# Value slabs on a second DMA queue: a decode-attention kernel with three slab buffers

## The chip, the cores and the metric

The kernel runs on one core of a Trainium2 chip. Its time is the device time of one execution, in microseconds (us), and smaller is better. A core has five engines with a program each, which meet only at semaphores: TensorE (PE) multiplies matrices, VectorE (DVE) and GpSimd (POOL) work element by element, ScalarE (ACT) evaluates functions, and SyncE (SP) does no arithmetic and here issues transfers. A transfer from the chip's main memory (HBM) into the core's own memory (SBUF) is an instruction on one of the engines, which puts the transfer on that engine's queue and goes on; 16 DMA engines then move the bytes, and a semaphore tells when all have landed. SP has a queue (q1 in the profile) and ACT has another (q10).

## The reference

The result is a gated mix of one decode step of attention over a cache and of a small feed-forward network, for two batch rows `b`, in float32:

```python
q = (x @ wq)                          # 640 -> 32 heads x 128
scores = einsum("bhqd,bhkd->bhqk", q, k_cache) * Dh**-0.5     # 4096 cached keys per head
p = softmax(scores)
o = einsum("bhqk,bhkd->bhqd", p, v_cache)
a = o.reshape(B, 1, 32 * 128) @ wo    # -> 640
b = silu(x @ w1) @ w2                 # 640 -> 1728 -> 640
g = sigmoid((x * gate_w).sum(-1))
return g * a + (1 - g) * b
```

Keys and values are 134 MB each, the weights 30 MB together. Every byte is used once.

## The kernel before

**Items.** The attention is cut into 16 items, numbered `i` from 0 to 15: a group of four heads and one batch row each (group `i // 2`, row `i % 2`). The keys of an item are 128 rows of 64 KB, a slab of 8.39 MB that fills one of three equal buffers; its values are another such slab. The text calls them k0 to k15 and v0 to v15. Three loads of weights use the same buffers: the pair of slabs wq (with w1 behind it), the slab mid (two groups of wo, and w2) and, last, the slab end (the other six groups of wo).

**The stream.** The loads have one fixed order, the list `stream` (lines 80 to 88): wq 0, wq 1, k0, v0, k1, v1, ..., k5, v5, k6, mid, k7, v6, k8, v7, ..., k15, v14, v15, end. From k7 on the values are one item behind the keys. `pump` (line 126) goes along this list and issues a load as soon as the entry three places before it has been spent; `spend` marks an entry as done at the place in the program where its last reader stands, and calls `pump`. So the loads stand in the engines' programs at the places of `spend`, and each then waits on the chip for the reader that frees its buffer. The pool `slabs` deals out its three buffers; where two are free at once, it decides which load gets which. In the kernel before, all slab loads are SP's, and SP issues them in the order of the list.

**One item.** Each step is a function. `products(i)`: DVE and POOL multiply the key slab by the query in place, each a part of the columns (lines 346 and 343). `scores(i)`: DVE sums each product over the head dimension (line 354), which spends k_i. `peak(i)`: the negative maximum, four short DVE operations (359 to 363). `weights(i)`: four exps on ACT (369). `total(i)`: PE adds the exps up (380). `values(i)`: 64 matmuls on PE of the exps with the value slab (395), which spends v_i. `combine(i)`: DVE scales the result by the inverse total (407), and PE adds it to the group's rows (417). `turn`: after every second item, DVE sums and transposes a finished group (428, 429). `project` and `merge`: PE multiplies groups by wo (226, 240).

**Order.** The order on each engine is that of the program. The main loop runs i from 0 to 16: products(i), total(i−1), the inverse (`invert`), values(i−1), scores(i), peak(i), weights(i), the query of the next group, then combine(i−1) and turn. So on DVE combine(i−1), which waits for values(i−1), stands ahead of products(i+1). Ahead of the loop stand the gate, the queries (PE, line 314, which spends wq 0) and the first half of the feed-forward network; x and the gate row are loaded by ACT (144, 145). Behind the loop stand the projections with the end slab and one store of 5 KB (479).

**Who frees what.** In the first half v_i takes the buffer of k_(i−1) and waits for scores(i−1) on DVE, and k_i takes that of v_(i−2) and waits for values(i−2) on PE. In the second half v_i takes the buffer of k_i and waits for scores(i), and k_i takes that of v_(i−3) and waits for values(i−3).

Of the kernel before, what the change touches and what calls it, by code (L numbers as in the profile page):

```python
# [15 lines left out]
def tile_gated_decode(  # L16
# [12 lines left out]
    nc = tc.nc  # L29
# [63 lines left out]
    def load_wo(grp, t):  # L93
        at = WO_AT[grp][1]
        src = wo[grp * QD : (grp + 1) * QD, :].rearrange("(p n) d -> p (n d)", n=Q)
        cuts = (0, Q * D - D, Q * D) if grp == HQ - 1 else (0, Q * D)
        for c0, c1 in zip(cuts, cuts[1:]):
            nc.sync.dma_start(t[:, at + c0 : at + c1], src[:, c0:c1])

    def load(what, n, t):  # L100
        if what in ("k", "v"):
            hq, b = items[n]
            src = (kc if what == "k" else vc)[b, Q * hq : Q * hq + Q]
            src = src.rearrange("h s d -> (h s d)").rearrange("(p c) -> p c", p=P)
            step = SLAB // 2 if (what, n) == ("v", N - 1) else SLAB
            for c in range(0, SLAB, step):
                nc.sync.dma_start(t[:, c : c + step], src[:, c : c + step])
        elif what == "wq":
            src = wq.rearrange("(p j) n -> p (j n)", j=J)
            if n == 0:  # L110
                nc.sync.dma_start(t, src[:, :SLAB])
            else:
                nc.sync.dma_start(t[:, :W1_AT], src[:, SLAB:])
                nc.sync.dma_start(t[:, W1_AT : W1_AT + J * F], w1.rearrange("(p j) f -> p (j f)", j=J))
        elif what == "mid":
            for grp in range(WO_MID):
                load_wo(grp, t)
            nc.sync.dma_start(t[:, : FR * D], w2[:FM, :].rearrange("(p n) d -> p (n d)", n=FR))
            nc.sync.dma_start(
                t[:, W2T_AT : W2T_AT + HD], w2[FM:, :].rearrange("r (e c) -> (r e) c", e=2)  # L120
            )
        else:
            for grp in range(WO_MID, HQ):
                load_wo(grp, t)

    def pump():
        while nxt[0] < len(stream):
            m = nxt[0]
            if m >= SLOTS and stream[m - SLOTS] not in spent:
                return  # L130
            t = slabs.tile([P, SLAB], F32, tag="slab", name=stream[m][0])
            load(*stream[m], t)
            T[stream[m]] = t
            nxt[0] += 1
# [38 lines left out]
    for i in range(2):  # L173
        t = const.tile([P, NG, 32], F32, name=f"pz{i}")
# [328 lines left out]
```

## Time and profile before

| | |
|---|---|
| median of 3 runs | 700.46 us (699.23 to 700.59) |
| profiled execution: its time | 700.36 us |
| its span, first to last instruction | 698.5 us |
| bytes read from HBM | 298.26 MB, 427 GB/s over the span |
| busy: DVE / PE / POOL / ACT | 469.4 / 224.7 / 265.7 / 37.8 us |
| TensorE clock granted, mean | 0.667 |

How the lines are read. The rows of slices cut the span in 40 equal parts of 17.5 us; a digit is the busy share in tenths, and 9 is 90% or more. A row of the queue table has the queue's packets, megabytes and the time its packets took as a share of 16 engines' span. A row of the timeline has the start in us, the length in us, the engine (SPq and ACTq are the issues of transfers), the line, the operation, what it writes and what it reads, and in brackets the engine's idle time before it and what ended that. A row of groups has the busy time, the mean in ns of one, and the idle time of the engine before such instructions. A row of windows has the stretch, its length, the busy time of each engine, the granted clock, the share of the DMA engines and GB/s. The landing of a transfer is read from the first instruction that waited for it.

### The profile page before, as it was taken

How to read it: one execution, taken by the hardware profiler on the slowest of the kernel's cores; microseconds unless marked ns; L12 is line 12 of the kernel's file. 1: busy time of each engine (PE TensorE's matmuls, PEld its weight loads, DVE VectorE, ACT ScalarE, POOL GpSimd, SP SyncE). 2: the span in 40 equal slices, each digit the busy share in tenths (PEclk: the TensorE clock that was granted, in tenths of full speed). 3: DMA queues.
4: the chain of work that ended last, by engine and by line, in shares of the span. 5: the costliest groups of instructions: out<-in, count | busy, mean ns of one | idle time of the engine just before them, and what ended most of it. 6: DMA issues, size and time to landing. Idle time of an engine off the chain costs nothing.

```text
span 698.5 us, 3649 instructions
## 1 busy us (share of the span) xinstructions
PE 224.7 (32%) x1516; PEld 73.4 (11%) x1516; DVE 469.4 (67%) x215; ACT 37.8 (5%) x143; POOL 265.7 (38%) x27
## 2 busy tenths in 40 slices
PE   1630050605032150752240506050321406060477
PEld 1210010101010010210010102010100102010113
DVE  2016949394967869496949597695949495786901
ACT  0000000101010100101010101000010101010010
POOL 1006244270907153353618080624426080715300
PEclk9985565756657575877575757566565757566689
DMA  9999999999999999999999999999999999999995
GB/s 410 408 454 424 420 455 439 420 428 440 443 428 432 424 448 435 413 446 439 424 440 432 439 428 440 428 435 435 436 432 432 435 424 448 428 440 424 425 416 248
DMA packets 6803, 298.51 MB, mean 427 GB/s; under 512 B 759, under 2 KB 895, under 8 KB 1154
## 3 DMA queue, kind: packets, MB, share of 16 engines
q1 hardware_dynamic: 6780, 298.26, 98.8%
q8 instruction: 12, 0.20, 0.1%
q14 instruction: 5, 0.04, 0.0%
q10 hardware_dynamic: 6, 0.01, 0.0%
HBM read 298.26 MB, written 0.01 MB: 427 GB/s over the span
## 4 chain that ended last, share of the span: by engine, by line
DMA 60%; DVE 24%; PE 13%; another core or an unknown queue 1%; ACT 0%; issue 0%; SPq 0%; DVEq 0%; ACTq 0%
DMA k<-in_A_k_cache_dram 34%; DMA v<-in_A_v_cache_dram 20%; DVE s L354 15%; PE pv L395 10%; DVE k L346 8%; DMA wq<-in_B_w_dram 5%; PE acc L226 2%; PE orow L417 1%; PE hr L257 1%; DVE osb L407 0%; ACT pz L369 0%; PE tot L380 0%; DVE rg L388 0%; DVE m L359 0%
## 5 line engine op out<-in xcount | busy, mean ns | idle before, releaser
L343 POOL TENSOR_TENSOR k<-k,qsb 128x7680 f32<-128x7680 f32 x16 | 262.8, 16422 | 386.4 <-DMA k<-in_A_k_cache_dram 386.4
L354 DVE TENSOR_REDUCE s<-k 128x68 f32<-128x8704 f32 (+1 forms) x32 | 276.3, 8677 | 0.0
L346 DVE TENSOR_TENSOR k<-k,q 128x8704 f32<-128x8704 f32 x16 | 147.5, 9221 | 136.5 <-DMA k<-in_A_k_cache_dram 126.4
L395 PE MATMUL pv<-v,pz 128*32 128x512 f32 x1024 | 145.2, 730 | 247.9 <-DMA v<-in_A_v_cache_dram 247.9
L395 PEld LDWEIGHTS pv<-v,pz 128*32 128x32 f32 x1024 | 36.5, 131 | 342.7 <-issue 226.7
L417 PE MATMUL orow<-osb,pick 128*128 128x512 f32 x32 | 22.8, 800 | 117.4 <-DVE osb L407 117.4
L369 ACT ACTIVATE pz<-s,nb 32x128 f32<-32x128 f32 x64 | 25.5, 398 | 585.2 <-DVE nb L363 584.6
L407 DVE SCALAR_TENSOR_TENSOR osb<-pv,rg,own 128x512 f32<-128x512 f32 x16 | 12.0, 748 | 21.3 <-PE pv L395 21.2
L276 DVE STREAM_TRANSPOSE turned<-hr 128x416 f32<-128x416 f32 (+1 forms) x2 | 0.8, 414 | 29.4 <-PE hr L265 29.4
L380 PE MATMUL tot<-rs,fold 128*128 128x1 f32 x32 | 5.8, 251 | 43.9 <-ACT pz L369 43.9
L417 PEld LDWEIGHTS orow<-osb,pick 128*128 128x128 f32 x32 | 5.8, 226 | 127.1 <-DVE osb L407 127.1
L331 PE MATMUL q<-qrow,spread 128*128 128x128 f32 x32 | 7.2, 359 | 26.1 <-DVE tot L385 17.8
L314 PE MATMUL qr<-wq,xz 128*32 128x512 f32 x80 | 11.5, 745 | 8.7 <-DMA wq<-in_A_wq_dram 8.7
L428 DVE TENSOR_REDUCE row<-orow 128x128 f32<-128x512 f32 x8 | 5.5, 692 | 11.6 <-PE orow L417 11.6
L380 PEld LDWEIGHTS tot<-rs,fold 128*128 128x128 f32 x32 | 7.2, 235 | 55.3 <-ACT pz L369 52.3
L226 PE MATMUL acc<-mid,hT 128*17 128x320 f32 x52 | 10.0, 556 | 7.6 <-DMA mid<-in_B_w_dram 7.6
L369 ACT ACTIVATION_READ_ACCUMULATOR pz<-s,nb 32x1 f32 x64 | 11.8, 184 | 0.0
L226 PE MATMUL acc<-end,oP 128*17 128x320 f32 (+2 forms) x128 | 11.2, 367 | 0.0
L331 PEld LDWEIGHTS q<-qrow,spread 128*128 128x128 f32 x32 | 5.4, 240 | 33.0 <-issue 22.9
L478 DVE COPY ot<-acc 128x160 f32<-128x160 f32 x1 | 0.3, 324 | 11.0 <-PE acc L226 11.0
L257 PE MATMUL hr<-wq,xz 128*32 128x416 f32 x40 | 5.6, 681 | 3.7 <-DMA wq<-in_B_w_dram 3.7
L197 DVE COPY xz<-xT 128x10 f32<-128x10 f32 x1 | 0.2, 168 | 9.1 <-PE xT L189 9.1
(59 smaller groups left out, 69.0 us busy)
## 6 DMA issues: line engine op xcount, KB each, us to landing
v<-in_A_v_cache_dram SPq DMA_DIRECT2D x2, 4096.0 KB, 38.3
end<-in_A_wo_dram SPq DMA_DIRECT2D x5, 1280.0 KB, 21.3
wq<-in_B_w_dram SPq DMA_DIRECT2D x1, 4320.0 KB, 37.2
mid<-in_B_w_dram SPq DMA_DIRECT2D x1, 4160.0 KB, 26.8
mid<-in_A_wo_dram SPq DMA_DIRECT2D x2, 1280.0 KB, 17.4
wq<-in_A_wq_dram SPq DMA_DIRECT2D x1, 2048.0 KB, 26.5
end<-in_A_wo_dram SPq DMA_DIRECT2D x1, 960.0 KB, 27.0
end<-in_A_wo_dram SPq DMA_DIRECT2D x1, 320.0 KB, 27.3
```

The source lines that it names most:

```text
L226: nc.tensor.matmul(dst[32 * n : 32 * n + m, :], lhsT, w[:, n * width : (n + 1) * width], start=(count[to] == 0), stop=(count[to] == total_ ...
L257: nc.tensor.matmul(rows[32 * c : 32 * c + 32, :QF], xz[:, j, :], w[:, j, c * QF : (c + 1) * QF], start=(j == 0), stop=(j == J - 1),)
L314: nc.tensor.matmul(ps[u][32 * q : 32 * q + 32, :], xz[:, j, :], w[:, u * half : (u + 1) * half, q, :], start=(j == 0), stop=(j == J - 1),)
L331: nc.tensor.matmul(qps[hq][:, b, :], spread[:, b, :], qrow[:, hq, :], start=True, stop=True)
L343: nc.gpsimd.tensor_mul(k[:, CV:, :], k[:, CV:, :], qsb[hq][:, b, None, :].to_broadcast([P, C - CV, DH]))
L346: nc.vector.tensor_mul(k[:, :CV, :], k[:, :CV, :], qps[hq][:, b, None, :].to_broadcast([P, CV, DH]))
L354: nc.vector.reduce_sum(S[i][:, c0:c1], k[:, c0:c1, :], axis=AX.X)
L369: nc.scalar.activation(pz[i % 2][lo:hi, :, 4 * q : 4 * q + 4], S[i][lo:hi].rearrange("p (g c) -> p g c", c=4), AF.Exp, bias=M[i][lo:hi], s ...
L380: nc.tensor.matmul(t[:, :1], fold.rearrange("p a q c -> p (a q c)"), R[i], start=True, stop=True)
L395: nc.tensor.matmul(PV[i][32 * q : 32 * q + 32, :], pz[i % 2][:, gr, :], v[:, gr, :], start=(gr < 4), stop=(gr >= NG - 4),)
L407: nc.vector.scalar_tensor_tensor(osb, PV[i].rearrange("p (c d) -> p c d", d=DH), R[i], own[:, :, None].to_broadcast([P, 4, DH]), op0=ALU.mult,
L417: nc.tensor.matmul(PO[hq].rearrange("p c d -> p (c d)"), pick[:, HB * (1 - b) : HB * (1 - b) + P], osb.rearrange("p c d -> p (c d)"), star ...
```

## The change

Value loads are issued by ACT on its queue instead of by SP. Keys and weights stay with SP.

```diff
             for c in range(0, SLAB, step):
-                nc.sync.dma_start(t[:, c : c + step], src[:, c : c + step])
+                eng = nc.sync if what == "k" else nc.scalar
+                eng.dma_start(t[:, c : c + step], src[:, c : c + step])
```

A line is added, so lines behind 107 count one more in the changed kernel. In the built program, 17 loads (v15 is loaded in two halves) move from SP's program into ACT's. Each v_i stands on ACT at the place of the `spend` that lets it out: v0 ahead of the query copies, v1 to v5 and v6 to v14 each ahead of the four exps of `weights` of the item that was just scored, v15 behind v14. On SP the keys and the weights follow each other directly.

The waits of most loads are as before. From v7 on the pool, which there has two free buffers for two loads at the same place, deals them the other way round:

| load | waits before | waits after |
|---|---|---|
| v1 to v6 | DVE, scores(0) to scores(4), scores(6) | the same |
| k2 to k8, mid | PE, values(0) to values(5), middle; DVE, scores(5) | the same |
| v7 to v14 | DVE, scores(i) | PE, values(i−1) |
| k9 to k15 | PE, values(i−3) | DVE, scores(i−2) |
| v15 | PE, values(13) | DVE, scores(14) |
| end | DVE, scores(15) | PE, values(14) |

So in the changed kernel v6 to v14 and the end slab use one and the same buffer, and k7 to k15, with mid and v15, the other two. The last piece of the end slab also waits for the first half of v15, with which it shares a semaphore.

## The prediction

> **What bounds the kernel now.** I read the slices first, then the queue table, then the timeline around the slab loads.
>
> ```profile
> span 698.5 us, 3649 instructions
> DMA  9999999999999999999999999999999999999995
> ...
> DMA packets 6803, 298.51 MB, mean 427 GB/s; under 512 B 759, under 2 KB 895, under 8 KB 1154
> ...
> q1 hardware_dynamic: 6780, 298.26, 98.8%
> ...
> q10 hardware_dynamic: 6, 0.01, 0.0%
> ```
>
> Transfers bound it: SP's queue (q1) keeps the 16 DMA engines at 98.8% of the span, and only the last slice is not full. ACT's queue (q10) carries nothing but x and the gate. A load of 128 rows makes 128 packets and, as the 759 small ones show (47 such loads times 16 are 752), a completion mark on each of 16 engines. So moving the same bytes can win almost nothing; the question is whether the DMA engines, with two queues, ever run empty.
>
> ```profile
> 0.74 0.39 SPq L111 DMA_DIRECT2D wq<-in_A_wq_dram  x1
> 1.30 0.23 ACTq L145 DMA_DIRECT2D wq<-in_gate_w_dram  x1
> 10.59 2.33 PE L189 MATMUL xT<-ident,wq 3*128 3x3 f32 x10 [10.59 <-DMA wq<-in_gate_w_dram]
> 22.96 11.55 PE L314 MATMUL qr<-wq,xz 128*32 128x512 f32 x80 [8.66 <-DMA wq<-in_A_wq_dram]
> 32.85 0.33 SPq L107 DMA_DIRECT2D v<-in_A_v_cache_dram  x1
> 58.18 9.22 DVE L346 TENSOR_TENSOR k<-k,q 128x8704 f32<-128x8704 f32 x1 [10.06 <-DMA k<-in_A_k_cache_dram]
> 67.44 17.28 DVE L354 TENSOR_REDUCE s<-k 128x68 f32<-128x8704 f32 x2
> 84.74 0.33 SPq L107 DMA_DIRECT2D v<-in_A_v_cache_dram  x1
> 88.43 9.53 PE L395 MATMUL pv<-v,pz 128*32 128x512 f32 x64
> 97.00 9.22 DVE L346 TENSOR_TENSOR k<-k,q 128x8704 f32<-128x8704 f32 x1 [11.23 <-DMA k<-in_A_k_cache_dram]
> 98.03 0.33 SPq L107 DMA_DIRECT2D k<-in_A_k_cache_dram  x1
> ```
>
> What to see: k0 has landed at 58.18, DVE has its scores at 84.72 (26.6 later), and v1, which takes k0's buffer, is issued at once, 12.3 us before k1 lands (97.00). That lead is what keeps the engines fed with three buffers.
>
> ```profile
> 391.53 0.33 SPq L107 DMA_DIRECT2D v<-in_A_v_cache_dram  x1
> 392.60 0.33 SPq L107 DMA_DIRECT2D k<-in_A_k_cache_dram  x1
> 394.58 0.69 DVE L428 TENSOR_REDUCE row<-orow 128x128 f32<-128x512 f32 x1 [1.22 <-PE orow L417]
> 403.30 9.22 DVE L346 TENSOR_TENSOR k<-k,q 128x8704 f32<-128x8704 f32 x1 [7.59 <-DMA k<-in_A_k_cache_dram]
> 422.71 9.64 PE L395 MATMUL pv<-v,pz 128*32 128x512 f32 x64 [27.63 <-DMA v<-in_A_v_cache_dram]
> ...
> 430.07 0.33 SPq L107 DMA_DIRECT2D v<-in_A_v_cache_dram  x1
> 432.41 0.33 SPq L107 DMA_DIRECT2D k<-in_A_k_cache_dram  x1
> 442.00 9.22 DVE L346 TENSOR_TENSOR k<-k,q 128x8704 f32<-128x8704 f32 x1 [8.83 <-DMA k<-in_A_k_cache_dram]
> ```
>
> The second half: v8 and k10 are issued a microsecond apart, on scores(8) and values(7), while k9 is still in transfer. One period is 442.00 − 403.30 = 38.7 us for two slabs, 19.35 us each (8.39 MB, 434 GB/s). Each DMA engine carries 8 of a slab's 128 rows, 2.42 us a row.
>
> ```profile
> 636.24 9.22 DVE L346 TENSOR_TENSOR k<-k,q 128x8704 f32<-128x8704 f32 x1 [6.34 <-DMA k<-in_A_k_cache_dram]
> 663.01 3.48 SPq L98 DMA_DIRECT2D end<-in_A_wo_dram  x7
> 674.82 6.44 PE L395 MATMUL pv<-v,pz 128*32 128x512 f32 x32 [4.29 <-DMA v<-in_A_v_cache_dram]
> 683.20 9.07 PE L226 MATMUL acc<-end,oP 128*17 128x320 f32 x72
> 695.80 0.69 SPq L479 DMA_DIRECT2D out_dram<-ot  x1
> ```
>
> The tail: the end slab, queued last, lands last.
>
> ```profile
> 690.00:698.50 8.50, 4.76 (x88) 2.53 (x84) 0.32 (x1) 0.42 (x1) 0.00 (x0) 0.95 0.15 60
> ```
>
> The engines carry it for 0.15 of the last 8.5 us (the column before GB/s), so to about 691.3, and some 7 us follow. The out row puts a bound on a transfer's fixed cost: 695.80 to the span's end is 2.7 us for 5 KB. I take 2.65 in all, of which 0.95 lies between issue and first row and 1.7 between last row and use.
>
> **The change part by part.** *Issue slots.* 17 value loads leave SP and join ACT at about 0.33 us each, 5.6 us. ACT is idle beside them:
>
> ```profile
> L369 ACT ACTIVATE pz<-s,nb 32x128 f32<-32x128 f32 x64 | 25.5, 398 | 585.2 <-DVE nb L363 584.6
> ```
>
> So they cost nothing. Were that cover gone, it would be 5.6 us. What stands behind a waiting load on ACT is the next weights (four exps, 2 us), whose reader, PE, waits for the value slab anyway. SP loses the same slots and waits for keys alone.
>
> *How two queues share.* No run here has two slab streams, but the start has two queues. The gate row, issued on ACT at 1.53, is used at 10.59, in the middle of the 8 MB weight load queued before it (used at 22.96). x and gate make six entries on q10 by the queue table (three rows, three completion marks); if a row of x and the gate's row meet on one engine, four of them stand there in line, and four turns against rows of 2.42 us are 9.7 us: 1.5 + 9.7 = 11.2 against 10.59 measured. So I take it that an engine serves the two queues in turn, one row each: two slab loads together run at half speed each. With that rule, the waits of the built program and the durations above I walk the loads forward.
>
> The Trainium skill ("DMA: Bandwidth & Descriptors", "Queues, rings and completion order") says the same of the turns, but that one holds a whole packet of some 9 to 17 descriptors, which could be all 8 rows of a slab with their mark. The gate row speaks for single rows; by the packet rule the time would be that of the first rival.
>
> *Start.* v0 is issued at 33 as before, but now shares with k0 rather than waiting behind it. v0's 8 rows all go before k0's last, so k0 is ready 19.35 us later, at 77.5. Scores(0) end 26.6 later at 104.1, and v1's first row is at 105.0. k1's last row has gone at 97.00 − 1.7 = 95.3, since the bytes before it are the same; k2 waits for values(0), behind scores(0). Nothing is left to move: a hole of 9.7 us. Through items 1 to 6 the walk finds at most 0.5 us more: value and key loads overlap, each lands later, and each next issue still finds the other queue busy.
>
> *The buffers, from v7 on.* Here two loads are requested at one place in the code with two free buffers, and the built program deals them out otherwise than before: each of v7 to v14 takes the buffer of the value load before it (waits for values(i−1) on PE), and each of k9 to k15 that of the key load two before (waits for scores(i−2)). So values have one buffer, keys two. A value load can't be in transfer while the values before it are read: each must land (1.7), be read (8.5 to 9.6 by the rows above, 9.0 taken) and be issued anew (0.95 and some 0.3), 12 us in which only keys can move.
>
> The walk repeats every two items. v7 is used by 425.4; only then does DVE pass combine(7) and the turn of a finished head group (3 us), products and scores take 27, and k11 goes out at about 456.3. Meanwhile v8 starts at 426.6, shares with k10's last rows for some 7 us and is gone at 451.1. DVE holds both key slabs, PE needs v8 to land: a hole of 5.2 us. In the next item k11 and v9 overlap, k12 comes in time, and there is none. So two items take 82.8 instead of 77.4 us, with three holes (behind v8, v10, v12): 15.6 us.
>
> *End.* After k15 the only slabs left are v14, v15 and end. v14 waits for values(13); v15's buffer (k14's) has been free since scores(14), but it stands behind v14 in ACT's order. v13's last row goes at 660.8, v14's first row comes 1.7 + 9.0 + 0.3 + 0.95 later: 11.9 us of hole. The tail behind the end slab stays as it is, 0.
>
> *Sum.* 9.7 + 0.5 + 15.6 + 11.9 = 37.7 us. The profiled execution took 700.36, 0.1 from the median of 700.46, so 738. Bounds: with 0.7 and 2.7 us for the landing instead of 1.7 the walk gives +32 and +44, with values at 8 and 10 us +34 and +42; rows of 2.40 or 2.44 us move it by under 2. Both kinds together give its own range, 728 to 750.
>
> **The rivals.** *Whole loads in turn, or the later holes absorbed.* If an engine finishes a load before it changes queue, k0 still waits out v0, 9.7 us; but a later value load is done in one slab's time, half a period sooner, and the walk then finds no hole: 710. The same comes out if buffers turn out not to bind. Against it: the gate row. 0.14.
>
> *Service in order of issue across queues.* k0 then keeps its place and the start costs nothing; the one value buffer still costs 2.1 to 2.6 us in every second late item, under a microsecond in those between and 11.6 at the end, together 20: 720. Against it: the gate row again, in use 12 us before the load issued ahead of it. 0.05.
>
> *One queue gets more turns.* If ACT's goes first each time, the walk finds three holes of 10 us in the first three items, and k15 lands behind all other slabs but one, so that its products and scores (27 us) stand at the very end, some 25 us longer: 756. Nothing in the rows of before speaks for such an order. 0.05.
>
> *Faster: two queues move more bytes per second.* It would have to make up for the holes, 37.7 us of 698.5, so the rate must rise from 434 to over 459 GB/s at one point, the transfers themselves.
>
> ```profile
> GB/s 410 408 454 424 420 455 439 420 428 440 443 428 432 424 448 435 413 446 439 424 440 432 439 428 440 428 435 435 436 432 432 435 424 448 428 440 424 425 416 248
> ```
>
> No slice passes 455, and high ones stand beside low ones (408, 454, 424), as when packets fall to one side of a slice's edge; the engines already count as full. At 465 GB/s all the time it would be about 690. 0.03. The Trainium skill ("DMA: Bandwidth & Descriptors", "Specifications") gives a ceiling of 435 GB/s, which the 434 here agrees with; that would leave nothing to gain.
>
> *No change.* Order of service by issue, and buffers that never bind: 700.4. 0.02.
>
> **How the numbers follow.** My forecast, holes at start, late items and end, has 0.71: 738. Left out of 710 to 750 are the 756 case, faster, no change, and tails of the forecast and the first rival, together some 0.18. About 0.2% (1.4 us) is what a measurement here tells from no change. Only the no-change case lies within it, and only the rate case below it: faster 0.03, same 0.02, slower 0.95.
>
> **What will show it.** Right: DVE's first products on k at about 77 instead of 58.18; the DMA row below 9 in the slices at 94 to 104, near 453, 536, 619 and from 661 to 672; the share of q1 about half, q10 the other, together some 94%; v loads issued on ACT right after PE's values, from v7 on; v14 and v15 issued together near 672; the end slab last, near 731. Wrong on sharing: k0 at 58, or v0 used long before k0. Wrong on buffers: a v and a k load issued within 2 us of each other all through the second half, as now. Most likely to upset it: a fixed cost of a transfer other than 2.65 us, which counts at every hole.

## The result, and the profile after

The changed kernel takes 746.46 us (745.48 to 747.54, 4 runs) beside 700.45 for the kernel before: a ratio of 1.0665, 95% interval 1.0653 to 1.0677. The ratio is taken over all executions and is not exactly the quotient of the two medians. The changed kernel is 46.0 us slower; 37.7 were forecast, with 738 for the time and a range of 710 to 750.

The page of the changed kernel, with the slices of the DMA engines and its queues:

```profile
span 745.3 us, 3645 instructions
DMA  9999949997999999999999997999989996975995
GB/s 394 452 405 447 450 172 448 397 451 338 448 397 447 450 392 447 417 448 429 436 441 429 426 443 296 397 450 450 394 339 447 419 429 282 450 338 241 433 418 235
...
q1 hardware_dynamic: 4332, 164.04, 51.3%
q10 hardware_dynamic: 2454, 134.23, 41.9%
```

The unbroken row of nines now has dents in six places. The two queues together keep the engines at 93.2%, where one kept them at 98.8%, with the same megabytes. The dents in the changed kernel's windows, with GB/s as the last column:

```profile
90.00:110.00 20.00, 2.80 (x14) 1.09 (x18) 19.85 (x7) 1.96 (x8) 17.05 (x2) 0.50 0.50 203
...
175.00:195.00 20.00, 7.50 (x48) 2.60 (x52) 17.66 (x10) 1.96 (x8) 9.95 (x2) 0.59 0.86 360
200.00:300.00 100.00, 25.18 (x146) 8.23 (x147) 76.63 (x30) 6.44 (x26) 34.52 (x3) 0.61 0.99 428
450.00:470.00 20.00, 11.30 (x70) 3.46 (x70) 12.98 (x7) 1.02 (x5) 0.00 (x0) 0.64 0.67 276
532.00:552.00 20.00, 10.56 (x69) 3.43 (x70) 13.34 (x7) 0.70 (x3) 0.00 (x0) 0.64 0.77 315
614.00:634.00 20.00, 9.46 (x68) 2.98 (x68) 15.35 (x7) 0.09 (x1) 0.00 (x0) 0.64 0.65 266
660.00:680.00 20.00, 9.87 (x66) 2.42 (x66) 4.78 (x7) 0.57 (x3) 15.75 (x1) 0.69 0.51 207
730.00:745.30 15.30, 11.57 (x137) 5.21 (x136) 1.43 (x3) 0.42 (x1) 0.00 (x0) 0.97 0.46 194
```

Between the holes the rate is what it was (428 over 100 us). At 434 GB/s a stretch of 20 us with 203 lacks 20 × (1 − 203/434) = 10.6 us of transfer, whether the engines were empty or slow; the six come to 10.6, 3.4, 7.3, 5.5, 7.7 and 10.5, together 45.0. Each of these is uncertain by a microsecond or two, since a window may cut through the rows of 64 KB; their sum stands well beside the span's 46.8 us more.

The timeline of the changed kernel around the holes:

```profile
77.53 9.22 DVE L347 TENSOR_TENSOR k<-k,q 128x8704 f32<-128x8704 f32 x1 [24.12 <-DMA k<-in_A_k_cache_dram]
97.02 16.48 POOL L344 TENSOR_TENSOR k<-k,qsb 128x7680 f32<-128x7680 f32 x1 [2.95 <-DMA k<-in_A_k_cache_dram]
104.10 0.36 ACTq L108 DMA_DIRECT2D v<-in_A_v_cache_dram  x1
...
185.07 16.52 POOL L344 TENSOR_TENSOR k<-k,qsb 128x7680 f32<-128x7680 f32 x1 [10.05 <-DMA k<-in_A_k_cache_dram]
185.76 0.33 ACTq L108 DMA_DIRECT2D v<-in_A_v_cache_dram  x1
...
422.12 9.39 PE L396 MATMUL pv<-v,pz 128*32 128x512 f32 x64 [34.52 <-DMA v<-in_A_v_cache_dram]
431.58 0.34 ACTq L108 DMA_DIRECT2D v<-in_A_v_cache_dram  x1
434.61 9.18 DVE L347 TENSOR_TENSOR k<-k,q 128x8704 f32<-128x8704 f32 x1
458.47 9.98 PE L396 MATMUL pv<-v,pz 128*32 128x512 f32 x64 [24.02 <-DMA v<-in_A_v_cache_dram]
461.33 0.33 SPq L108 DMA_DIRECT2D k<-in_A_k_cache_dram  x1
...
669.17 8.75 PE L396 MATMUL pv<-v,pz 128*32 128x512 f32 x64 [32.83 <-DMA v<-in_A_v_cache_dram]
677.99 1.32 ACTq L108 DMA_DIRECT2D v<-in_A_v_cache_dram  x3
700.23 8.58 PE L396 MATMUL pv<-v,pz 128*32 128x512 f32 x64 [18.38 <-DMA v<-in_A_v_cache_dram]
708.87 3.31 SPq L98 DMA_DIRECT2D end<-in_A_wo_dram  x7
742.61 0.68 SPq L480 DMA_DIRECT2D out_dram<-ot  x1
```

k0 is used at 77.53 instead of 58.18. k1 has landed by 97.02, as before, but v1 is asked for only at 104.10, when scores(0) are done: in the kernel before it was asked for 12.3 us ahead of k1's landing, now 7.1 us behind. In the second half PE's values(7) end at 431.5, and in that instant v8 is issued; v8 lands at 458.47, and the next load of any kind is k11 at 461.33. At the end v13 lands at 669.17, and v14 and v15 are issued together at 677.99, right after values(13).

### The profile page after: what moved, and what is told of

It reads as the page before. It is cut to its first block, busy times and chain, and to the rows that moved or that the text cites. A ratio compares the mean times of both kernels' runs of the same rounds, so it can differ in the third digit from the quotient of the medians.

```text
span 745.3 us, 3645 instructions
## 1 busy us (share of the span) xinstructions
PE 225.0 (30%) x1516; PEld 71.6 (10%) x1516; DVE 468.7 (63%) x215; ACT 37.8 (5%) x143; POOL 266.0 (36%) x27
## 3 DMA queue, kind: packets, MB, share of 16 engines
q1 hardware_dynamic: 4332, 164.04, 51.3%
q10 hardware_dynamic: 2454, 134.23, 41.9%
## 4 chain that ended last, share of the span: by engine, by line
DMA 61%; PE 18%; DVE 15%; another core or an unknown queue 3%; issue 1%; ACT 0%; SPq 0%; DVEq 0%; ACTq 0%
DMA v<-in_A_v_cache_dram 42%; PE pv L396 14%; DMA k<-in_A_k_cache_dram 14%; DVE s L355 9%; DMA wq<-in_B_w_dram 6%; DVE k L347 5%; PE acc L227 1%; PE hr L258 1%; PE orow L418 1%; DVE osb L408 0%; ACT pz L370 0%; PE tot L381 0%; DVE m L360 0%; DVE turned L277 0%
## 5 line engine op out<-in xcount | busy, mean ns | idle before, releaser
L332 PE MATMUL q<-qrow,spread 128*128 128x128 f32 x32 | 5.6, 299 | 6.5 <-DVE tot L386 6.5
L227 PEld LDWEIGHTS acc<-end,oP 128*17 128x17 f32 (+1 forms) x128 | 5.1, 98 | 6.4 <-issue 6.1
```

The lines of the kernel that those rows point to most:

```text
L227: nc.tensor.matmul(dst[32 * n : 32 * n + m, :], lhsT, w[:, n * width : (n + 1) * width], start=(count[to] == 0), stop=(count[to] == total_ ...
L332: nc.tensor.matmul(qps[hq][:, b, :], spread[:, b, :], qrow[:, hq, :], start=True, stop=True)
```

## The experiments

Each kernel's median stands beside that of the kernel before on the same chip (699.8 to 700.3). Edits are shown against the changed kernel, but for one that starts from the kernel before. Where a kernel has three fixed buffers, the line of the three pools is shown in the first experiment only.

### The start alone

Three pools of one buffer each replace the pool of three, so that entry m of the stream takes buffer m mod 3 and all waits are those of the kernel before. Only v0 goes to ACT.

```diff
-    slabs = ctx.enter_context(tc.tile_pool(name="slabs", bufs=SLOTS))
+    slabs = [ctx.enter_context(tc.tile_pool(name=f"slab{s}", bufs=1)) for s in range(SLOTS)]
...
-            t = slabs.tile([P, SLAB], F32, tag="slab", name=stream[m][0])
+            t = slabs[m % SLOTS].tile([P, SLAB], F32, tag="slab", name=stream[m][0])
...
-                eng = nc.sync if what == "k" else nc.scalar
+                eng = nc.scalar if what == "v" and n == 0 else nc.sync
```

> The start by itself: three fixed buffers, v0 alone on ACT, every other load on SP. My theory: k0 is used at 77 to 78, one hole of 9.7 to 10.7 us after k1, and nothing else since one queue follows: 709 to 712 us. If the hole after k3 (4 us in the changed kernel) also comes from the start alone: up to 715. Rival 'the start costs less than its hole, the later order wins some back': 703 to 707.

Measured: 710.97 us against 700.32, ratio 1.0154 (1.0140 to 1.0168), so 10.7 us for one load on the other queue. Its windows show one hole and full rate behind it:

```profile
90.00:110.00 20.00, 2.88 (x14) 1.10 (x18) 19.85 (x7) 1.96 (x8) 17.12 (x2) 0.50 0.52 210
110.00:300.00 190.00, 60.97 (x396) 19.56 (x392) 138.63 (x54) 10.91 (x43) 68.98 (x5) 0.65 1.00 433
300.00:690.00 390.00, 124.98 (x800) 38.40 (x792) 289.57 (x112) 21.08 (x84) 164.21 (x10) 0.65 1.00 434
```

The first term of the sum (9.7 us) is shown, and the smaller hole near 185 is not part of it. Its queue rows (94.9% and 2.7% of a span of 708.1 us) say that the packets took 691.1 us, 1.0 more than the 98.8% of 698.5 us before; this is taken up with the sum below.

### How the queues share

One column of v0 is copied by DVE as soon as v0 has landed.

```diff
+    mark = const.tile([P, 1], F32, name="mark")
+    nc.vector.tensor_copy(mark, T["v", 0][:, :1])
     for i in range(N + 1):
```

> The changed kernel with one added DVE copy of one column of v0, ahead of the first products, where DVE is idle: it starts when v0 has landed. My theory (one row of each queue in turn): v0 and k0 run together from 33 on, v0 is read at 70 to 74, k0 at 77 to 78. Rival 'an engine finishes a load before it changes queue': v0 at about 56, k0 at 77. Rival 'in order of issue': v0 at about 77, k0 at 58. The time stays at 746.

```profile
76.25 0.15 DVE L457 COPY mark<-v 128x1 f32<-128x1 f32 x1 [22.28 <-DMA v<-in_A_v_cache_dram]
77.55 9.22 DVE L347 TENSOR_TENSOR k<-k,q 128x8704 f32<-128x8704 f32 x1 [1.15 <-DMA k<-in_A_k_cache_dram]
```

v0, issued 30 us behind k0, lands 1.3 us ahead of it: both ran side by side to the end. Whole loads in turn (56) and service in order of issue (k0 at 58) are out.

The 70 to 74 that I expected are missed by 2 us, and yet single rows in turn are right. The trace keeps a record of every packet, with its queue, size, start and length. From 45 to 70 us 81 rows of 64 KB start on SP's queue and 80 on ACT's, so neither queue gets more turns. On 14 of the 16 engines v0's last row has ended by 71.3, as the rule says. But on 12 of them the completion mark comes only at 73.2 to 73.7, which fits a turn of its own behind one more row of k0 (2.42 us). On two engines v0's last row ends at 75.7, and the semaphore waits for these. The time was 745.2 in its one execution.

### The buffers with two queues

The changed kernel with the three fixed buffers, all value loads on ACT:

```diff
-            t = slabs.tile([P, SLAB], F32, tag="slab", name=stream[m][0])
+            t = slabs[m % SLOTS].tile([P, SLAB], F32, tag="slab", name=stream[m][0])
```

> The changed kernel, but the three buffers are three pools and entry m of the stream takes buffer m mod 3, so that the loads wait as in the kernel before: v_i for scores(i), k_i for values(i-3). All value loads stay on ACT. My theory: the hole after k1 (9.7 us) stays, the late holes are gone: 710 to 716 us, the upper end if items 1 to 6 hold another 4 us as the changed kernel's profile suggests. Rival 'two slab streams at once are slow whatever the buffers': about 746. Rival 'the start costs nothing': about 700.

Measured: 717.65 (715.25 to 721.02), ratio 1.0256 (1.0216 to 1.0296), above the 710 to 716 expected. Of 46 us, 28 go with the buffers alone; the forecast had 15.6 + 11.9 = 27.5 for that.

The same part from the other side: v0 to v6 on SP, so the start and the first items are those of the kernel before; v7 to v15 on ACT, and the pool deals the buffers again (v7 to v14 in one).

```diff
-                eng = nc.sync if what == "k" else nc.scalar
+                eng = nc.sync if what == "k" or n <= MID + 1 else nc.scalar
```

> The late part by itself: v0 to v6 on SP, v7 to v15 on ACT, and the pool deals the buffers as in the changed kernel, v7 to v14 in one buffer. Against e8 (707.4), which has the same queues and fixed buffers, the difference is the one value buffer with two queues. My theory: three holes of 5 us, one of 12 and what e8 loses: 727 to 737. Rival 'the buffer only matters when the early loads have already spent the lead': 707 to 712.

Measured: 729.48 (726.77 to 731.29), ratio 1.0414 (1.0388 to 1.0439), 29.2 us; its windows hold the largest hole at the end, as in the changed kernel:

```profile
475.00:495.00 20.00, 10.47 (x66) 2.56 (x66) 12.64 (x8) 1.90 (x8) 16.70 (x2) 0.68 0.76 315
...
640.00:660.00 20.00, 9.62 (x66) 2.40 (x66) 11.77 (x8) 1.22 (x5) 15.53 (x1) 0.71 0.41 161
```

So the value buffer needs no spent lead at the start to cost. The kernel with the same queues and fixed buffers (late values on ACT, below) loses 7.6 us, so here the one value buffer is worth some 22 of the 29 us, less than the 28 beside early values on ACT.

### The buffers with one queue

The kernel before, all loads on SP, with three pools and the changed kernel's deal:

```diff
+    def slot_of(m):
+        what, n = stream[m]
+        if what == "k" and n > MID + 2:
+            return 0 if n % 2 == 0 else 1
+        if what == "v" and n > MID + 1:
+            return 0 if n == N - 1 else 2
+        return 2 if what == "end" else m % SLOTS
...
+            t = slabs[slot_of(m)].tile([P, SLAB], F32, tag="slab", name=stream[m][0])
```

> The kernel before, all loads on SP, but from v7 and k9 on the buffers are dealt out as in the changed kernel: v7 to v14 follow each other in one buffer, k9 to k15 alternate in the other two, and end takes the value buffer. My theory: with one queue the loads keep their order and are requested some 11 us before the engines need them, values(i-1) end within 2 us of scores(i), so 700 to 702 us: the one value buffer costs only together with the second queue. Rival 'one value buffer costs by itself, since a value load can't be in transfer while the values before it are read': about 727.

Measured: 700.23 against 700.00, ratio 1.0001 (0.9992 to 1.0011). No change. The same three buffers in the same deal cost 28 us with two queues and nothing with one. With one queue the values are done within 2.4 us of the scores (the timeline of before, 430.07 and 432.41), and a slab asked for then still stands behind others: here v8 is issued at 432.02, and k9, ahead of it on the queue, is used at 442.11, 10 us later.

### The other queue by itself

Three fixed buffers, every slab load on ACT in the order of the stream, x and the gate on SP:

```diff
-                eng = nc.sync if what == "k" else nc.scalar
+                eng = nc.scalar
...
-                nc.sync.dma_start(t, src[:, :SLAB])
+                nc.scalar.dma_start(t, src[:, :SLAB])
...
-    nc.scalar.dma_start(xg[:B], x.rearrange("b s d -> (b s) d"))
+    nc.sync.dma_start(xg[:B], x.rearrange("b s d -> (b s) d"))
```

> Three fixed buffers; all slab loads, keys, values and weights, are issued by ACT in the order of the stream, on one queue, and x and the gate by SP: the same single queue as before, but the other one. If ACT's queue, its issue slots between the exps or its program order cost anything, it shows here: over 703. My theory, that only the meeting of two queues costs: 700 to 702 us.

```profile
q10 hardware_dynamic: 6768, 298.26, 98.9%
```

Measured: 699.16 against 699.82, ratio 0.9990 (0.9981 to 0.9998). ACT's queue is as good as SP's, and its issue slots among the exps cost nothing. A tenth of a per cent is less than this measurement can tell from no change, so this is no better kernel.

### What is left without either hole

v0 on SP and three fixed buffers; 16 of 17 value loads stay on ACT.

```diff
-                eng = nc.sync if what == "k" else nc.scalar
+                eng = nc.sync if what == "k" or n == 0 else nc.scalar
```

> Both of the two former edits: v0 on SP, three fixed buffers, 16 of 17 value loads on ACT's queue. My theory: no hole is left, the DMA engines stay full, 699 to 702 us, no change from the kernel before although almost all value loads still share the engines with the keys. Rival 'ACT's queue, its issues or the interleaving of rows cost something by themselves': over 706. Rival 'two queues move more bytes per second': under 698.

Measured: 710.43 (704.24 to 713.83), ratio 1.0139 (1.0081 to 1.0197). My theory was wrong here: some 10 us remain, and single executions lie 10 us apart, where the kernels with one queue stay within 2. The profiled one (708.05, a span of 706.1) loses 1.8 us between 130 and 140, where v2 is issued at 133.28 with little left to move, and nothing in the long late stretch:

```profile
130.00:140.00 10.00, 4.98 (x20) 1.84 (x24) 8.06 (x7) 2.33 (x9) 3.19 (x1) 0.53 0.87 354
375.00:600.00 225.00, 58.91 (x392) 17.94 (x396) 170.78 (x65) 12.22 (x49) 96.86 (x6) 0.63 1.00 434
```

Its queue rows show more of it:

```profile
q1 hardware_dynamic: 4476, 172.43, 56.8%
q10 hardware_dynamic: 2310, 125.84, 41.5%
```

Together these are 694.1 us of 706.1, so the same packets took 4.0 us longer than in the kernel before. Its packet records have three groups of some 15 slow rows, near 134, 213 and 366 us, each where a value load starts as the load before it runs out.

So I supposed that the rest stood in items 1 to 6, where k_i lands later for the rows of v_i in between. Two kernels split it, both with fixed buffers:

v7 to v15 on ACT (the late values):

```diff
-                eng = nc.sync if what == "k" else nc.scalar
+                eng = nc.sync if what == "k" or n <= MID + 1 else nc.scalar
```

> Three fixed buffers as in e2; v0 to v6 on SP behind the keys, only v7 to v15 on ACT. It halves what is left in e3 (about 10 us over the kernel before, with no v0 at the start and no shared value buffer). My theory of that rest: as long as v_i is issued while k_i is still in transfer, k_i lands later by the rows of v_i that go in between, and the 12 us by which a load is requested ahead shrinks to nothing in items 1 to 6 (small holes of 1 to 2 us near 137, 292), while from item 7 on the rate is full (434 GB/s from 375 to 600 us in e3) and only the end loses some 3 us. So here 702 to 705 us. Rival 'two slab streams slow the engines everywhere': 706 to 708.

v1 to v6 on ACT (the early values):

```diff
-                eng = nc.sync if what == "k" else nc.scalar
+                eng = nc.scalar if what == "v" and 0 < n <= MID + 1 else nc.sync
```

> The other half: three fixed buffers, v1 to v6 on ACT, v0 and v7 to v15 on SP. My theory: the lost lead of items 1 to 6 stands here, 703 to 708 us, and the small holes near 137 and 292 are seen again. Rival 'the rest is at the end': 700 to 701.

Measured: late 707.41 (701.28 to 709.19), ratio 1.0089 (1.0058 to 1.0120); early 704.59 (702.45 to 708.79), ratio 1.0079 (1.0051 to 1.0108). Both halves cost, and both vary. The early values came out as expected, the late ones at the rival's 706 to 708: that the early items hold it all is refuted. The late kernel's profiled execution was its fastest (701.28), so no profile shows where 707 comes from; this part stays open.

The changed kernel with v0 given back to SP, buffers as the pool deals them:

```diff
-                eng = nc.sync if what == "k" else nc.scalar
+                eng = nc.sync if what == "k" or n == 0 else nc.scalar
```

> The changed kernel with one load given back: v0 is issued by SP behind k0, all other value loads by ACT. The waits of the late loads are those of the changed kernel (one value buffer from v6 on). My theory (queues served row by row, and the value buffer): k0 is used at 58 again, the hole after k1 is gone, the late holes (about 5, 5, 5 and 12 us) stay: 727 to 733 us. Rival 'sharing alone does it, buffers never bind': about 700. Rival 'the late part does it all': about 746.

Measured: 742.44 (734.82 to 743.59), ratio 1.0583 (1.0530 to 1.0636). Only some 4 us come back, and I had expected 13 to 19. Its DMA slices:

```profile
DMA  9999999999999999999999995999699995975996
```

The hole at the start is gone, and k0 is used at 58.87 again. But the dents of the second half are deeper: 5, 6, 5 and 5 tenths, where the changed kernel has 7, 8, 6 and 5. By its packet records the four late holes are empty for 8.2, 7.0, 7.4 and 11.9 us, beside 5.7, 4.2, 5.9 and 10.5. With v1 on ACT k1 comes at 107.22 (97.00 in the kernel before), so the keys run later against the values from there on; that this deepens the late holes is not shown. The parts are not independent, and 10.7 us for v0 by itself is not what it costs among the rest.

### Two details of the late part

v15 on SP, where it doesn't stand behind v14:

```diff
-                eng = nc.sync if what == "k" else nc.scalar
+                eng = nc.sync if what == "k" or n == N - 1 else nc.scalar
```

> The changed kernel with both halves of v15 issued by SP, so that they no longer stand behind v14 in ACT's order; their buffer has been free since scores(14). As the prediction words it, v15's place behind v14 is why 12 us pass empty near 670: then the hole closes, and 734 to 736 us. Rival, the same walk done again for this case: the hole only moves, for v15 now shares with v14 and the end slab, which follows in v14's buffer, has to wait for values(14) with no other transfer left: 744 to 748, no change, with a hole of 12 us near 708 instead of 670.

```profile
660.00:680.00 20.00, 10.80 (x66) 2.62 (x66) 2.67 (x6) 1.38 (x6) 16.46 (x1) 0.66 0.96 414
700.00:720.00 20.00, 11.91 (x84) 3.68 (x88) 9.95 (x8) 1.96 (x8) 0.00 (x0) 0.72 0.37 147
```

Measured: 744.33, ratio 1.0661 (1.0601 to 1.0722), as the changed kernel. The hole near 670 closes, and 13 us open near 710, ahead of the end slab, which waits for values(14) in the one value buffer. ACT's order was the place of the hole, not its cause.

The query copy ahead of the waiting load. In the changed kernel the waits show it:

```profile
DVE k L347 <- ACT qsb L334: 8.4, 4, 2.1
```

```diff
+            if i + 1 < N and items[i + 1][1] == 0:
+                query(items[i + 1][0])
             scores(i)
             peak(i)
             weights(i)
-            if i + 1 < N and items[i + 1][1] == 0:
-                query(items[i + 1][0])
```

> The changed kernel with the query of the next group computed ahead of scores(i): on ACT its copy then stands ahead of the waiting value load and the four exps, not behind them. In the changed kernel products of every second item wait 2.1 us for that copy. Rival 'the copy behind the load costs time': faster by up to 8 us (four times 2.1), 738 to 744. My walk: products, scores and so the key loads of even items come 2 us sooner and are used up sooner beside the value load, so each of the three late holes grows by 2 to 3 us: 748 to 754.

Measured: 747.95 (746.39 to 752.52), ratio 1.0708 (1.0672 to 1.0743). Not faster, so the four waits of 2.1 us cost nothing. The 748 to 754 of the walk are not clearly met either: the median stands at their lower edge, and the interval meets that of the changed kernel.

## Why the prediction was right

**Bound and sign.** Transfers bound the kernel, nothing was to be won, and most of the loss is time in which the DMA engines have nothing to move. The rule of single rows in turn is borne out by the packet records (81 and 80 rows in 25 us). The mean rate between holes, 428 to 434 GB/s, is that of one queue, and the rival of a higher rate falls. The Trainium skill ("DMA: Bandwidth & Descriptors", "Issuing engines are not separate DMA queues") says that queues of several engines interleave on the same 16 engines and save only issue time. The trace agrees that nothing is saved; what is lost by the interleaving is on top of that.

**Start: 9.7 us, right.** k0 was to be ready at 77.5 and is used at 77.53; scores(0) at 104.1, v1 issued at 104.10. By landings the hole is 104.10 − 97.02 + 2.65 = 9.7, and alone it costs 10.7.

**Items 1 to 6: 0.5 us, mis-sized.** By landings it is 185.76 − 185.07 + 2.65 = 3.3 us. v3 was asked for when scores(2) were done, and k2 had been used only at 158.6. The prediction does not show this part of its walk, so which of its landings came too early stays open. Two things that it left out make a shared load land later: the mark's own turn, and the longer first rows told below. The early sharing costs 4.8 us by itself in the kernel with early values on ACT.

**Late holes: 15.6 us, right in kind and nearly in size.** v8's landing to k11's issue is 461.33 − 458.47 = 2.9, with 2.65 some 5.5 us. The rows for v10 and v12:

```profile
541.21 9.58 PE L396 MATMUL pv<-v,pz 128*32 128x512 f32 x64 [24.40 <-DMA v<-in_A_v_cache_dram]
543.70 0.33 SPq L108 DMA_DIRECT2D k<-in_A_k_cache_dram  x1
...
624.54 8.87 PE L396 MATMUL pv<-v,pz 128*32 128x512 f32 x64 [23.49 <-DMA v<-in_A_v_cache_dram]
627.94 0.33 SPq L108 DMA_DIRECT2D k<-in_A_k_cache_dram  x1
```

These are 5.1 and 6.1, so 16.7 together, in the places where they were forecast, behind v8, v10 and v12. From v8 to v10 to v12 are 82.7 and 83.3 us, where the walk had 82.8. (Its 82.8 is 5.4 above 77.4, and not the 5.2 that the sum takes three times.)

**End: 11.9 us, right in size, its wording not.** 677.99 − 669.17 + 2.65 = 11.5. That v15 stood behind v14 was told as part of the reason, and the run with v15 on SP shows that it isn't.

**The sum: 37.7 forecast, 46.0 measured.** By landings the holes are 9.7 + 3.3 + 16.7 + 11.5 = 41.2. The rest of the profiled span's 46.8 lies in two terms that the prediction put at nothing.

The first is a slower start behind each hole. The queue rows give 98.8% of 698.5 us before, 690.1, and 51.3% and 41.9% of 745.3 us after, 694.6: the same megabytes kept the engines busy 4.5 us longer. The packet records show where. Most rows of 64 KB take 2.42 us, as the prediction has it, but 134 of 4096 took over 2.6 us, beside 26 before. Some 120 of them stand in eight groups of 13 to 16: one at the kernel's own start, which the kernel before has too, one behind each of the six holes, and one near 264, where v5 starts as k5 ends. The first row that each engine moves there takes some 3 us, so each of the seven restarts costs 0.6 to 0.75 us on top of the empty time. Why it does is not shown.

The second is the tail. By the last row of the windows the engines carry the end slab for 0.46 of 15.3 us, to 737.0, and 8.3 us follow, where in the kernel before 7.2 follow 691.3. That is 1.1 us more, and no run looks into it. 41.2 + 4.5 + 1.1 = 46.8; that they meet to the tenth is luck, as each part is uncertain by half a microsecond or more.

The fixed cost of a transfer, named as most likely to upset the sum, did not: v14, alone on the engines, takes 700.23 − 677.99 = 22.24 us from issue to use, 2.9 beyond a slab's 19.35, of which the longer first row is about 0.7. The terms do not stand by themselves, though, as the sum has it: without the start's hole the late holes are larger (v0 given back to SP). One sentence was incomplete: behind a waiting load on ACT stands not only weights but also the next query copy, which DVE and POOL wait for; it costs nothing.

## What to carry to other kernels

One queue does more than issue: it keeps transfers in the order in which they will be needed. On two queues a slab that is needed later takes half the rate from one that is needed now, and with few buffers the later request that follows leaves the engines empty, with a slow first row (some 3 us for 2.42) behind each hole; look at how far ahead of need each load is asked for (here 12 us) before splitting a stream that is already at full rate. When loads change engine, look also at which buffer the pool gives them: here 28 of the 46 us hung on it with two queues, and nothing with one.

## What the runs showed that I had not expected

Some kernels with slabs on two queues vary from one execution to the next: 704 to 714 us (v0 on SP, fixed buffers) and 701 to 709 (late values on ACT), beside 698.9 to 699.6 with all loads on ACT and 699.4 to 701.2 for the kernel before on one chip. Two queues alone do not do it: the changed kernel (745.5 to 747.5) and the one with v0 alone on ACT (709.9 to 711.3) stay within 2.1 us. Each kernel has one profile, so where the executions differ is not shown.
